# Three transfers instead of five for each block of raw weights, and the inverse root of the norms by logarithm and exponential instead of a power: a fused attention and SwiGLU kernel

## The chip, the cores and the metric

The kernel runs on one core of one Trainium2 chip. The metric is the device time of one execution in microseconds; a smaller time is better. A core has TensorE (PE in the profile; PEld is its weight load), VectorE (DVE), ScalarE (ACT), GpSimd (POOL) and SyncE (SP). Each has its own queue of instructions, worked off in order, and waits for the others by semaphores. SP only begins transfers (DMAs) here; ScalarE and GpSimd can begin some too.

## The reference

```python
# 8 batches, 12 heads, 448 positions, 64 values a head
def rmsnorm(x, g):
    rms = np.sqrt(np.mean(x * x, axis=-1, keepdims=True) + 1e-06)
    return x / rms * g
q_n, k_n = (rmsnorm(q, g_q), rmsnorm(k, g_k))
scores = 1.0 / np.sqrt(64) * np.matmul(q_n, k_n.transpose(0, 1, 3, 2))
attn = np.exp(scores - np.max(scores, axis=-1, keepdims=True))
attn = attn / (np.sum(attn, axis=-1, keepdims=True) + 1e-09)
x = np.matmul(attn, v)         # then laid out as 3584 tokens x 768
# gate and value weights 768 x 1536, output weights 1536 x 768
g = x @ w_gate
return (g * (1.0 / (1.0 + np.exp(-g))) * (x @ w_val)) @ w_out
```

The step that the change touches is `1 / rms`, the inverse root, for each row of q and k.

## The kernel before

The three weights arrive as 64-bit numbers, and the kernel turns them into 32-bit numbers itself. The large products are not done as written. Each is cut into 3 x 3 blocks and done with 15 smaller products in place of 27; for that, sums and differences of blocks ("sides") are needed of the weights and of the tokens. So a piece of weights goes through a *conversion* (`convert`): a load of nine raw blocks, two ScalarE activations (L1129, L1133), six VectorE instructions that round the numbers (L1151 to L1163), twelve GpSimd sums and differences of blocks (L1182, L1185), and a transfer of all 15 sides to DRAM (L1210), to `up_sides` (gate and value weights) or `down_sides` (output weights). There are 24 conversions: 16 of gate and value weights, 8 of output weights. Four blocks (`BLOCKS`) are sides as they are, the other eleven are made. Later `load_sides` (L1271) fetches the sides in the order in which the products use them, five at a time for the hidden products and two at a time for the output products, with one transfer for each run of neighbours.

Attention works on 48 *pairs* (two heads of one batch each, six pairs a batch), twelve pairs for each block of two batches. For each pair (`attention(m)`) the queue of work is:

- q and k are loaded by four transfers each (L702), v by four (L718, L721);
- ScalarE squares both (L728), VectorE sums the squares of rows (L742), ScalarE swaps halves between partitions (L752), VectorE adds the two and a small constant (L756), which gives `ss`, 128 partitions x 28 sums;
- the inverse root `rr` of these 28 sums: one GpSimd power (L767);
- GpSimd multiplies k and q by `rr` (L778, one instruction each), VectorE transposes them (L794), ScalarE multiplies q by both gains (L797);
- TensorE makes scores (L823), ScalarE exponentials (L838), TensorE weighted sums (L899) and row sums of the exponentials (L930). In later blocks GpSimd and VectorE first add the exponentials up (L843, L849);
- a reciprocal (L965), its spread over partitions (L973 or L983), and the join and division into `xs` (L988, L991, L995). VectorE then makes the token sides (L1032, L1036).

The buffers of q and k hold two pairs, so the loads of a pair wait for the pair two before it.

The stages follow each other like this: twelve early pairs beside six conversions; the hidden products of block 0 (L1311, with their reads L1253 to L1259, Silu L1385 and the weighing L1388) beside the other 18 conversions; then in turn for each block the output products (L1485) mixed with the twelve pairs of the next block, and the hidden products of that block; at the end the output products of block 3 alone.

The order on every queue is not written by hand. The class `Order` takes pieces of work with an engine, an estimated duration, a due time and dependencies, simulates the engines with these estimates, and emits each engine's instructions in the order that the simulation chose. The chip then works each queue strictly in that order. A piece of ScalarE's may name a `mode`, the table set it needs; a change of mode is booked at 1.3 us. The estimates and lines that matter here:

```python
rr = add("POOL", 0.5, ready - 14.0, roots, after=[sums], uses=[("ss", m)], takes=[("rr", m)])
# scale: "POOL", 1.0 each;  transpose: "DVE", 0.62;  queries: "ACT", 0.65
loaded = add("SP", 2.5, when - 12.0, load, after=[staged.get(place), *wait], kb=1152, early=3.0)
```

`by_bank` is false for the first six conversions, those among the early pairs, and true for the other 18. The tables are set to hold logarithm and exponential together (`natural_log_exp_and_others`, loaded in `load_tables`, L552); Silu needs another set, loaded before L1385.

Of the kernel before, what the change touches and what calls it, by code (L numbers as in the profile page):

```python
# [477 lines left out]
def fast(  # L478
# [41 lines left out]
    nc = tc.nc  # L520
# [3 lines left out]
    P = 128  # L524
# [15 lines left out]
    const = ctx.enter_context(tc.tile_pool(name="const", bufs=1))  # L540
# [7 lines left out]
        rr=4, ws=2, **{x + str(i): 1 for x in "vw" for i in range(6)},  # L548
# [5 lines left out]
    order = Order(BUFS, dict(logarithms=load_tables))  # L554
    tiles = {}

    WORK, size = {}, 0
# [48 lines left out]
    FRESH = (2, 6, 8, 12, 9)  # L606


    UP_SUMS = (8, 1, 7, 13, 10, 14, 3, 5, 11, 0, 4)
    DOWN_SUMS = (1, 10, 14, 3, 11, 0, 4, 5, 8, 7, 13)  # L610
    BLOCKS = (6, 2, 12, 9)
    WS = 10 * NC2 * P
    up_sides = [dram.tile([P, 15, 2, NC2, P], F32, name=f"up_sides{g}") for g in range(NG)]
    down_sides = dram.tile([P, 15, 2, NG, P], F32, name="down_sides")
# [17 lines left out]
    minus_half = const.tile([P, 1], F32, name="minus_half")  # L632

# [31 lines left out]
    down_products = {}  # L665


    SCALE = 2.0**8
    SPREAD = 6.0

    NC = S // C
    clusters = {}
# [4 lines left out]
    def attention(m):  # L677
# [53 lines left out]
        for x in range(2):  # L731
# [3 lines left out]
                    after=[loaded[x], *squares], uses=[("qk", (m, x))] + [("t", m)] * x,  # L735
                    takes=[("t", m)] * (1 - x),
# [25 lines left out]
        )  # L762
        sums = add("ACT", 0.9, ready - 16.0, swap, after=[sums], uses=[("ss", m)])
        sums = add("DVE", 0.15, ready - 15.0, both, after=[sums], uses=[("ss", m)])

        def roots():
            nc.gpsimd.tensor_tensor(  # L767
                out=take("rr", m, [P, 2 * NC]), in0=tiles["ss", m][:, 0],
                in1=minus_half.to_broadcast([P, 2 * NC]), op=ALU.pow,
            )  # L770

        rr = add(
            "POOL", 0.5, ready - 14.0, roots, after=[sums], uses=[("ss", m)], takes=[("rr", m)]
        )

        def scale(x):
            rr = tiles["rr", m][:, ts(x, NC)].rearrange("p (c one) -> p c one", one=1)
# [18 lines left out]
        def queries():  # L796
# [7 lines left out]
            uses=[("t", m)],  # L804
# [298 lines left out]
    def convert(key, src, sums, to, when, place, by_bank):  # L1103

        rank = 20.0 if by_bank else 0.0

        def add(*what, **more):
            return order.add(*what, **dict(rank=rank, **more))

        raw, dst = places[place][:, 0 : 2 * VALUES], places[place][:, 2 * VALUES : PLACE]  # L1110
        words = raw.bitcast(U32).rearrange("p (n two) -> p n two", two=2)
        lo, hi = words[:, :, 0], words[:, :, 1]
        wait = [last_exp[0]] if place in (ES, PAIRS, GT[2]) else []

        def load():

            to = raw.bitcast(I64).rearrange("p (b f) -> p b f", f=P)
            for i, n, rows in ((0, 2, (1, 3, 0)), (2, 2, (0, 2, 2)), (5, 3, (0, 3, 1))):
                nc.sync.dma_start(to[:, i : i + n], src(slice(*rows[:2]), rows[2]))
            for i, k, n in ((4, 0, 0), (8, 2, 2)):  # L1120
                nc.sync.dma_start(to[:, i], src(k, n))

        loaded = add(
            "SP", 2.5, when - 12.0, load, after=[staged.get(place), *wait], kb=1152, early=3.0
        )
        bits = dst.bitcast(U32)
# [12 lines left out]

        def half(k):  # L1140
            part = ts(k, VALUES // 2)
            if not by_bank:
                return part, bits[:, part]
            bank_of = tiles[bank].rearrange("p b t -> p (b t)")
            return part, bank_of[:, 0 : VALUES // 2].bitcast(U32)

        def shift(k):
            if by_bank and k == 0:
                take(*bank, [P, 2, TB])
            part, to = half(k)  # L1150
            nc.vector.tensor_scalar(  # L1151
                out=to, in0=bits[:, part], scalar1=3, scalar2=None, op0=ALU.logical_shift_left
            )

        def sign(k):
            part, to = half(k)
            nc.vector.scalar_tensor_tensor(
                to, hi[:, part], 0x80000000, to, op0=ALU.bitwise_and, op1=ALU.bitwise_or
            )

        def round_part(k):
            part, to = half(k)
# [12 lines left out]
        b21, b31, b13, b23, b11, b12, b22, b32, b33 = (blocks[:, i] for i in range(9))  # L1175

        sides = places[place].rearrange("p (b f) -> p b f", f=P)[:, 7:22]
        at = {x: i for i, x in enumerate(sums)}
        w = {x: sides[:, i] for x, i in at.items()}

        def minus(to, one, two):
            return lambda: nc.gpsimd.tensor_tensor(out=to, in0=one, in1=two, op=ALU.subtract)  # L1182

        def plus(to, one, two):
            return lambda: nc.gpsimd.tensor_tensor(out=to, in0=one, in1=two, op=ALU.add)  # L1185

        def pair(x, i, j):
            return x[:, i : j + 1 : j - i]

        def twice(x):  # L1190
            return x.rearrange("p (one f) -> p one f", one=1).to_broadcast([P, 2, P])

        for us, op in (
            (0.79, plus(pair(sides, at[10], at[4]), pair(blocks, 5, 7), pair(blocks, 2, 8))),
            (0.79, plus(pair(sides, at[1], at[14]), twice(w[10]), pair(blocks, 0, 4))),
            (0.48, plus(w[14], w[14], b31)),
            (0.48, minus(w[13], b22, w[10])),
            (0.48, minus(w[8], w[4], b23)),
            (0.48, plus(w[7], b21, b22)),
            (0.48, minus(w[7], w[8], w[7])),  # L1200
            (0.48, minus(w[3], b13, b31)),
            (0.48, minus(w[5], b13, b21)),
            (0.48, plus(w[5], w[5], b11)),
            (0.79, minus(pair(sides, at[11], at[0]), pair(blocks, 7, 8), pair(blocks, 2, 3))),
            (0.48, plus(w[0], w[0], b31)),
        ):
# [66 lines left out]

    def place_of(x, part, sums):
        mine = [*(y for y in sums if y in part), *(y for y in BLOCKS if y in part)]
        return mine.index(x)

    def block(n):
        add = order.add
# [292 lines left out]


    nc.gpsimd.memset(many, SCALE)
    nc.gpsimd.memset(minus_half, -0.5)
    nc.gpsimd.memset(halves, 0.0)
    for x in range(2):
        nc.gpsimd.memset(halves[ds(D * x, D), x], SCALE)
# [7 lines left out]
    for i in range(P // C):  # L1586
# [95 lines left out]
```

## Time and profile before

| | us |
|---|---|
| median of 3 runs | 1596.77 (1596.45 to 1597.97) |
| the profiled execution | 1596.45 |
| its span, first to last instruction | 1594.7 |
| PE busy | 1468.6 (92%) |
| VectorE busy | 896.1 (56%) |
| ScalarE busy | 657.3 (41%) |
| GpSimd busy | 644.1 (40%) |
| mean granted TensorE clock | 0.965 of full speed |
| moved by DMA | 193.29 MB |

The profile is of one execution. A group's line gives the code line, the engine, the operation, output and inputs with their shapes, the count, the busy time in us and the mean of one in ns, and after the bar how long the engine had been idle just before these instructions and what ended most of that. In a line of the timeline come the start, the length, the engine and the code line, and in brackets the idle time before and its releaser. A line of the waits names the waiting engine and instruction, what it waited for, the sum in us, how often, and the longest. In the table of stages come the stretch and its length, then the busy time of each engine with its instructions, the granted TensorE clock, the DMA share (mean busy share of the 16 DMA engines) and GB/s.

### The profile page before, as it was taken

Reading aid. Unit: us, or ns where it says so; the run is one execution under the profiler, and the core shown is the slowest. Engines: PE = TensorE matmul, PEld = TensorE weight load, DVE = VectorE, ACT = ScalarE, POOL = GpSimd, SP = SyncE. Lnnn points to the kernel's source line nnn. Section 1 sums busy time; section 2 is a strip of 40 time slices with the busy share of each in tenths; the row PEclk is TensorE's granted clock in tenths of the full one; section 3 lists DMA queues with packets and bytes.
Section 4 is the critical chain, followed back from the end, with each engine's and each line's share of the span. In section 5 each row is a group of like instructions: output and inputs, shape, how many; then the busy total and the mean of one; then the engine's idle time right before and its main releaser. Section 6 shows DMA issues by size and latency. Waiting matters only on the chain.

```text
span 1594.7 us, 19324 instructions
## 1 busy us (share of the span) xinstructions
PE 1468.6 (92%) x6672; PEld 688.4 (43%) x6672; DVE 896.1 (56%) x1261; ACT 657.3 (41%) x1264; POOL 644.1 (40%) x517
## 2 busy tenths in 40 slices
PE   4787889996888899999998999999998989999998
PEld 1333445442333345544443345554443434555554
DVE  2566887775674754443676764334676673333543
ACT  4574344334656332134665432234665532222100
POOL 5786757647856510034476610033377620000000
PEclk9898999998998999999998999999999999999999
DMA  5664899982433242253344251253344343222235
GB/s 110 139 147 108 274 305 353 290 259 61 97 82 75 71 106 99 95 118 104 76 107 101 59 125 67 99 136 89 83 108 87 83 90 110 87 79 99 80 91 100
DMA packets 415920, 193.29 MB, mean 121 GB/s; under 512 B 324164, under 2 KB 397892, under 8 KB 409668
## 3 DMA queue, kind: packets, MB, share of 16 engines
q1 hardware_dynamic: 402688, 190.35, 44.6%
q10 hardware_dynamic: 12996, 1.61, 0.7%
q8 instruction: 55, 0.90, 0.2%
q14 instruction: 53, 0.43, 0.1%
q0 software_dynamic: 128, 0.00, 0.0%
HBM read 157.29 MB, written 34.60 MB: 120 GB/s over the span
## 4 chain that ended last, share of the span: by engine, by line
PE 54%; DVE 8%; issue 6%; ACT 4%; POOL 3%; SPq 2%; DMA 2%; DVEq 0%; ACTq 0%; POOLq 0%
PE mm L1311 17%; PE at L1311 17%; PE mm L1485 13%; PE st L823 3%; PE at L899 2%; ACT spare L983 2%; POOL sums L843 2%; DVE xs L1036 1%; DVE rd L965 1%; SPq L702 1%; DVE sums L849 1%; POOL work L778 1%; ACT es L838 1%; DVE work L794 1%; DVE xs L995 1%
## 5 line engine op out<-in xcount | busy, mean ns | idle before, releaser
L1311 PE MATMUL mm<-xs,ws 128*128 128x448 f32 x960 | 401.9, 541 | 7.9 <-DMA ws<-up_sides 4.3
L767 POOL TENSOR_TENSOR rr<-ss,minus_half 128x28 f32<-128x28 f32 x48 | 237.2, 4941 | 414.6 <-DVE ss L756 406.9
L1311 PE MATMUL at<-xs,ws 128*128 128x448 f32 x960 | 402.7, 542 | 1.4 <-DVE v L1257 1.0
L1311 PEld LDWEIGHTS mm<-xs,ws 128*128 128x128 f32 x960 | 181.7, 190 | 189.6 <-issue 175.5
L1311 PEld LDWEIGHTS at<-xs,ws 128*128 128x128 f32 x960 | 183.0, 191 | 183.1 <-issue 173.2
L823 PE MATMUL st<-work 64*64 64x448 f32 (+1 forms) x1536 | 174.8, 561 | 92.0 <-ACT work L797 60.5
L1485 PE MATMUL mm<-gt,ws 128*128 128x448 f32 x448 | 186.3, 568 | 0.0
L1485 PE MATMUL mm<-hs,ws 128*128 128x448 f32 x384 | 155.3, 556 | 0.0
L794 DVE STREAM_TRANSPOSE work<-work 128x448 f32<-128x448 f32 x96 | 60.7, 636 | 162.8 <-POOL work L778 156.7
L838 ACT ACTIVATE es<-st 128x896 f32<-128x896 f32 x129 | 114.7, 914 | 67.3 <-PE at L899 39.4
L843 POOL TENSOR_TENSOR sums<-es 128x896 f32<-128x896 f32 x36 | 76.0, 2110 | 160.9 <-ACT xs L988 61.3
L823 PEld LDWEIGHTS st<-work 64*64 64x64 f32 x1536 | 53.0, 143 | 181.2 <-ACT work L797 68.5
L1255 DVE TENSOR_TENSOR gt<-gt,mm 128x448 f32<-128x448 f32 x64 | 39.6, 618 | 159.3 <-PE mm L1311 158.3
L983 ACT COPY spare<-rd 32x224 f32<-32x224 f32 x288 | 108.1, 375 | 50.0 <-DVE rd L965 43.7
L1485 PEld LDWEIGHTS mm<-gt,ws 128*128 128x128 f32 x448 | 87.4, 200 | 93.5 <-issue 90.8
L1385 ACT ACTIVATE st<-gt 128x448 f32<-128x448 f32 x96 | 52.4, 547 | 181.4 <-DVE gt L1259 83.2
L899 PE MATMUL at<-es,v 64*64 64x448 f32 x1032 | 110.2, 541 | 5.7 <-DVE xs L991 5.5
L1485 PEld LDWEIGHTS mm<-hs,ws 128*128 128x128 f32 x384 | 73.0, 195 | 75.3 <-issue 74.1
L1253 ACT COPY gt<-mm 128x448 f32<-128x448 f32 x80 | 42.5, 532 | 146.3 <-PE mm L1311 146.3
L778 POOL TENSOR_TENSOR work<-work,rr 128x448 f32<-128x448 f32 x96 | 97.1, 1030 | 3.5
L1253 ACT COPY v<-at 128x448 f32<-128x448 f32 x96 | 51.0, 532 | 80.5 <-PE at L1311 79.6
L843 POOL TENSOR_TENSOR sums<-sums,es 128x896 f32<-128x896 f32 x36 | 79.6, 2212 | 2.7
(147 smaller groups left out, 1570.9 us busy)
## 6 DMA issues: line engine op xcount, KB each, us to landing
ws<-up_sides SPq DMA_DIRECT2D x32, 1024.0 KB, 5.0
ws<-down_sides SPq DMA_DIRECT2D x16, 1024.0 KB, 4.9
ws<-down_sides SPq DMA_DIRECT2D x28, 512.0 KB, 4.3
ws<-up_sides SPq DMA_DIRECT2D x16, 768.0 KB, 4.4
work<-in_q_dram SPq DMA_DIRECT2D x192, 56.0 KB, 2.4
work<-in_k_dram SPq DMA_DIRECT2D x188, 56.0 KB, 2.5
out_dram<-spare SPq DMA_DIRECT2D x168, 56.0 KB, 1.9
v<-in_v_dram SPq DMA_DIRECT2D x96, 96.0 KB, 2.4
```

The lines of the kernel that those rows point to most:

```text
L767: nc.gpsimd.tensor_tensor(out=take("rr", m, [P, 2 * NC]), in0=tiles["ss", m][:, 0], in1=minus_half.to_broadcast([P, 2 * NC]), op=ALU.pow,)
L778: nc.gpsimd.tensor_tensor(out=tiles["t", m][:, x], in0=tiles["qk", (m, x)], in1=rr.to_broadcast([P, NC, C]), op=ALU.mult,)
L794: nc.vector.transpose(to, tiles["t", m][:, x].rearrange("p c f -> p (c f)"))
L823: nc.tensor.matmul(st[ds(D * x, D), h, 0:n], tiles["KT", m][rows, ds(P * j + D * of_keys, D)], tiles["QT", m][rows, ds(Q * of_queries, n)] ...
L838: nc.scalar.activation(e, tiles["st", (m, j)][:, :, 0 : S * width(j) // P], AF.Exp)
L843: nc.gpsimd.tensor_tensor(out=to, in0=tiles["e", (m, 0)] if j == 1 else to, in1=e, op=ALU.add)
L899: nc.tensor.matmul(tiles["at", (m, x)][ds(D * h, D), queries], tiles["v", m][rows, j, h], tiles["e", (m, j)][rows, h], start=j == 0, stop= ...
L983: nc.scalar.copy(inv[ds(D * h + C * to, C), ts(x, Q)], tiles["rd", m][ds(D * h + C * x, C)])
L1253: nc.scalar.copy(to, ps)
L1311: nc.tensor.matmul(ps(), w[:, at, which, c], xs[:, SLOT[x], c], start=fresh and c == 0, stop=c == NC2 - 1, skip_group_check=True,)
L1385: nc.scalar.activation(take(*act, [P, 2, TB])[:, 0, 0:S], to, AF.Silu)
L1485: nc.tensor.matmul(banks[s][:, 0:S], w[:, at, s, g], where[x][:, g], start=fresh and g == 0, stop=g == NG - 1, skip_group_check=True,)
```

## The change

The inverse root is made by two ScalarE activations, logarithm and then exponential of minus half of it, and three VectorE instructions that improve the result by one step of iteration. The sums are scaled by a power of two before the logarithm, and the product of the gains (`gg`) makes up for it. The power and its constant `minus_half` go.

The nine blocks of a raw weight come in three transfers of three blocks instead of two of two blocks, one of three and two of one. For that the rounded blocks lie ahead of the raw ones instead of behind, in another order, and so do the 15 sides: `BLOCKS` first, then the sums, both reordered; `load_sides` and `place_of` follow, and the same twelve GpSimd sums are written with the new places. For the first six conversions (`by_bank` false) GpSimd begins the three transfers, with 3.0 us booked on its queue; for the others SP does, with 1.5 us for 2.5.

```diff
-    UP_SUMS = (8, 1, 7, 13, 10, 14, 3, 5, 11, 0, 4)
-    DOWN_SUMS = (1, 10, 14, 3, 11, 0, 4, 5, 8, 7, 13)
-    BLOCKS = (6, 2, 12, 9)
+    UP_SUMS = (10, 14, 3, 8, 1, 7, 13, 5, 11, 0, 4)
+    DOWN_SUMS = (3, 10, 14, 1, 11, 0, 4, 5, 8, 7, 13)
+    BLOCKS = (6, 9, 2, 12)
...
+    def inverse_root(m, sums, of, when, rank=0.0):
+        def estimate():
+            ss = of()
+            rr = take("rr", m, list(ss.shape))
+            nc.scalar.activation(rr, ss, AF.Ln, scale=GAIN**-2)
+            nc.scalar.activation(rr, rr, AF.Exp, scale=-0.5)
+
+        def improve():
+            ss, rr = of(), tiles["rr", m]
+            times = nc.vector.scalar_tensor_tensor
+            times(ss, rr, GAIN**-2, ss, op0=ALU.mult, op1=ALU.mult)
+            times(ss, ss, -0.5, rr, op0=ALU.mult, op1=ALU.mult)
+            times(rr, ss, 1.5, rr, op0=ALU.add, op1=ALU.mult)
+
+        first = order.add(
+            "ACT", 0.5, when, estimate, after=[sums], uses=[("ss", m)], takes=[("rr", m)],
+            mode="logarithms", rank=rank,
+        )
+        return order.add(
+            "DVE", 0.45, when + 1.0, improve, after=[first], uses=[("ss", m), ("rr", m)],
+            rank=rank,
+        )
...
-        def roots():
-            nc.gpsimd.tensor_tensor(
-                out=take("rr", m, [P, 2 * NC]), in0=tiles["ss", m][:, 0],
-                in1=minus_half.to_broadcast([P, 2 * NC]), op=ALU.pow,
-            )
-
-        rr = add(
-            "POOL", 0.5, ready - 14.0, roots, after=[sums], uses=[("ss", m)], takes=[("rr", m)]
-        )
+        rr = inverse_root(m, sums, lambda: tiles["ss", m][:, 0], ready - 14.0, rank)
...
-        raw, dst = places[place][:, 0 : 2 * VALUES], places[place][:, 2 * VALUES : PLACE]
+        dst, raw = places[place][:, 0:VALUES], places[place][:, VALUES:PLACE]
...
-            for i, n, rows in ((0, 2, (1, 3, 0)), (2, 2, (0, 2, 2)), (5, 3, (0, 3, 1))):
-                nc.sync.dma_start(to[:, i : i + n], src(slice(*rows[:2]), rows[2]))
-            for i, k, n in ((4, 0, 0), (8, 2, 2)):
-                nc.sync.dma_start(to[:, i], src(k, n))
+            queue = nc.sync if by_bank else nc.gpsimd
+            for at, n in ((slice(3, 8, 2), 0), (slice(0, 3), 1), (slice(8, 3, -2), 2)):
+                queue.dma_start(to[:, at], src(slice(0, 3), n))

         loaded = add(
-            "SP", 2.5, when - 12.0, load, after=[staged.get(place), *wait], kb=1152, early=3.0
+            "SP" if by_bank else "POOL", 1.5 if by_bank else 3.0, when - 12.0, load,
+            after=[staged.get(place), *wait], kb=1152, early=3.0,
         )
...
-        b21, b31, b13, b23, b11, b12, b22, b32, b33 = (blocks[:, i] for i in range(9))
-
-        sides = places[place].rearrange("p (b f) -> p b f", f=P)[:, 7:22]
-        at = {x: i for i, x in enumerate(sums)}
+        b12, b22, b32, b11, b33, b21, b23, b31, b13 = (blocks[:, i] for i in range(9))
+
+        sides = places[place].rearrange("p (b f) -> p b f", f=P)[:, 5:20]
+        at = {x: i for i, x in enumerate((*BLOCKS, *sums))}
...
-        for names, first in ((sums, 0), (BLOCKS, len(sums))):
-            here = sorted(names.index(x) for x in part if x in names)
-            if here:
-                size = len(here)
-                src = sides[:, ds(first + here[0], size)]
-                nc.sync.dma_start(to[:, ds(i, size)], src.rearrange("p x a b f -> p x (a b f)"))
-                i += size
+        here = sorted((*BLOCKS, *sums).index(x) for x in part)
+        while here:
+            size = next((n for n in range(1, len(here)) if here[n] != here[0] + n), len(here))
+            src = sides[:, ds(here[0], size)]
+            nc.sync.dma_start(to[:, ds(i, size)], src.rearrange("p x a b f -> p x (a b f)"))
+            i += size
+            here = here[size:]
...
-            out=gg, in0=gq2, scalar=8.0, in1=gk2, op0=ALU.mult, op1=ALU.mult
+            out=gg, in0=gq2, scalar=8.0 * GAIN**-2, in1=gk2, op0=ALU.mult, op1=ALU.mult
```

More of the change, by code (lines that the diff above doesn't have):

```diff
@@ L631, in fast @@
     gg = const.tile([P, 1], F32, name="gg")
-    minus_half = const.tile([P, 1], F32, name="minus_half")
     LEAD, PAIR = 14.0, 9.0
@@ L665, in fast @@
     down_products = {}
+    GAIN = 2.0**24
     SCALE = 2.0**8
     SPREAD = 6.0
+    def inverse_root(m, sums, of, when, rank=0.0):
[18 more added lines that the diff above has]
+        )
     NC = S // C
@@ L1187, in pair @@
         def pair(x, i, j):
-            return x[:, i : j + 1 : j - i]
+            return x[:, i : j + (1 if j > i else -1) : j - i]
         def twice(x):
@@ L1193, in convert @@
         for us, op in (
-            (0.79, plus(pair(sides, at[10], at[4]), pair(blocks, 5, 7), pair(blocks, 2, 8))),
-            (0.79, plus(pair(sides, at[1], at[14]), twice(w[10]), pair(blocks, 0, 4))),
+            (0.79, plus(pair(sides, at[10], at[4]), pair(blocks, 0, 2), pair(blocks, 8, 4))),
+            (0.79, plus(pair(sides, at[14], at[1]), twice(w[10]), pair(blocks, 3, 5))),
             (0.48, plus(w[14], w[14], b31)),
@@ L1203, in convert @@
             (0.48, plus(w[5], w[5], b11)),
-            (0.79, minus(pair(sides, at[11], at[0]), pair(blocks, 7, 8), pair(blocks, 2, 3))),
+            (0.79, minus(pair(sides, at[11], at[0]), pair(blocks, 2, 4), pair(blocks, 8, 6))),
             (0.48, plus(w[0], w[0], b31)),
@@ L1265, in load_sides @@
         i = 0
-        for names, first in ((sums, 0), (BLOCKS, len(sums))):
-            here = sorted(names.index(x) for x in part if x in names)
-            if here:
-                size = len(here)
-                src = sides[:, ds(first + here[0], size)]
-                nc.sync.dma_start(to[:, ds(i, size)], src.rearrange("p x a b f -> p x (a b f)"))
-                i += size
+        here = sorted((*BLOCKS, *sums).index(x) for x in part)
[5 more added lines that the diff above has]
+            here = here[size:]
     def place_of(x, part, sums):
-        mine = [*(y for y in sums if y in part), *(y for y in BLOCKS if y in part)]
-        return mine.index(x)
+        return [y for y in (*BLOCKS, *sums) if y in part].index(x)
     def block(n):
@@ L1574, in fast @@
     nc.gpsimd.memset(many, SCALE)
-    nc.gpsimd.memset(minus_half, -0.5)
     nc.gpsimd.memset(halves, 0.0)
```

## The prediction

> **What bounds the kernel now.** I read the page's summary by engine first (PE busy 92% of the span, GpSimd 40%), then cut the span into its stages and asked for busy time, granted clock and DMA share in each: the early pairs (0 to 157 us), the first hidden stage with most conversions of weights (157 to 361), the first stage in which attention pairs and output products alternate (361 to 580), and so on in turn.
>
> ```profile
> core 0: us, PE busy (x) PEld busy (x) DVE busy (x) ACT busy (x) POOL busy (x), PEclk, DMA share, GB/s
> 0.00:157.00 157.00, 107.69 (x1112) 45.76 (x1116) 79.91 (x125) 88.71 (x156) 109.93 (x97) 0.90 0.56 127
> 157.00:361.00 204.00, 193.33 (x576) 96.66 (x566) 163.60 (x244) 83.26 (x114) 125.80 (x240) 0.98 0.93 291
> 361.00:580.00 219.00, 185.08 (x1100) 76.88 (x1100) 136.38 (x165) 115.31 (x249) 137.48 (x60) 0.91 0.36 79
> ...
> 769.00:949.00 180.00, 168.72 (x1054) 73.28 (x1053) 121.43 (x149) 102.01 (x218) 104.41 (x46) 0.95 0.41 91
> ```
>
> PE is idle for 157 - 107.7 = 49.3 us in the first stage, 10.7 in the second, 33.9 in the third, and 11.3 in the stage at 769. The twin stage at 1136 to 1317 has 12.0, the other hidden stages (580, 949, 1317) under 1 each. So most of what can be won lies in stages one and three. Next I read who waits there (stage one, then stage three):
>
> ```profile
> DVE work L794 <- POOL work L778: 50.0, 20, 5.9
> PE st L823 <- ACT work L797: 37.5, 9, 18.5
> ```
>
> ```profile
> DVE work L794 <- POOL work L778: 33.8, 12, 5.2
> PE st L823 <- ACT work L797: 15.0, 2, 9.7
> ```
>
> PE waits for the queries (L797), they for the transposes (L794), these for GpSimd's scaling (L778), and in front of that stands the power:
>
> ```profile
> L767 POOL TENSOR_TENSOR rr<-ss,minus_half 128x28 f32<-128x28 f32 x48 | 237.2, 4941 | 414.6 <-DVE ss L756 406.9
> ```
>
> It takes 4.94 us on 28 elements a partition, although the planner that orders all queues books 0.5 us for it. So the transpose is queued on VectorE as if it were due at once, and whatever is queued behind it waits too. The timeline of one pair (GpSimd's line, then VectorE's, then PE's) shows it:
>
> ```profile
> 58.44 4.79 POOL L767 TENSOR_TENSOR rr<-ss,minus_half 128x28 f32<-128x28 f32 x1 [7.06 <-DVE ss L756]
> ...
> 64.28 0.65 DVE L794 STREAM_TRANSPOSE work<-work 128x448 f32<-128x448 f32 x1 [5.92 <-POOL work L778]
> ...
> 66.36 0.58 DVE L991 TENSOR_TENSOR xs<-xs,at 128x448 f32<-128x448 f32 x1
> ...
> 67.00 1.01 PE L899 MATMUL at<-es,v 64*64 64x448 f32 x2 [5.14 <-DVE xs L991]
> ```
>
> VectorE stands 5.92 us, the join L991 behind it comes late, and PE stands 5.14 us for that join. Stage three begins the same way:
>
> ```profile
> 362.79 4.80 POOL L767 TENSOR_TENSOR rr<-ss,minus_half 128x28 f32<-128x28 f32 x1 [15.23 <-DVE ss L756]
> ...
> 370.93 2.52 PE L823 MATMUL st<-work 64*64 64x224 f32 x16 [9.73 <-ACT work L797]
> ```
>
> Of PE's 9.73 us without work, 4.80 are the power. From 362.8 to 528.7 the twelve powers follow each other every 15.1 us, and one turn near 452 can be followed: GpSimd's two sums (4.4), VectorE's own sum and a read (1.9), row sums (1.1), ScalarE's swap (0.9), VectorE's combination and L756 (2.2), the power (4.8), one scaling (0.9), about 16 us. The power is a third of that loop.
>
> **The inverse root.** Removed: 48 powers, 237.2 us of GpSimd. Added for each pair: two ScalarE activations of 28 elements a partition (nearest row: a copy of 32x28, 212 ns, so 0.42), three VectorE instructions of the shape of L756 (median 189 ns, mean 316, so 0.57 to 0.95), and two more crossings between engines (58.36 to 58.44 in the rows above, 0.08, so 0.2). From L756 to the first scaling that makes 1.2 to 1.6 us; I take 1.5 for 4.94, a gain of 3.4 a pair. That is the best end. The other end: the new ScalarE pieces can stand behind two exponentials (2 x 0.91) and the VectorE pieces behind a reciprocal (1.5), and then 1.5 + 1.8 + 1.5 = 4.8 gains nothing. I take the gain's end, because the new costs are planned at 0.5 and 0.45, near those rows, so what is queued behind them arrives when it can run, which was not so for the power.
>
> Stage one: the nine waits of PE for the queries are one of 18.5 at the start and eight that sum to 19.0 (2.4 each). The first shrinks by 3.4, the eight by some 2 each: 20 us. Ends: 0, and 3.4 + 19.0 + the 5.1 of L991 = 27.5.
>
> Stage three: the loop falls to 15.1 - 3.4 = 11.7 us a pair, under what PE needs (185.1 / 12 = 15.4), so PE is next. It should then idle as at 769 (11.3) plus the start, 9.7 - 3.4 = 6.3: 185.1 + 17.6 = 202.7, a gain of 16. The granted clock is 0.91 here and 0.95 at 769; if the closer work brings it to 0.95, PE's 185.1 become 177.3, 8 more. Together 24; ends 0 and 39 (as short as the stage at 769, 180).
>
> The alternating stages at 769 and 1136: PE waits 4.0 for the queries in each. I take 3 each, 6 in all; ends 0 and 8. Stage two has no pairs, and the tail after 1317 has neither.
>
> Against this stand tables. Logarithm and exponential share the table set that the exponentials use, but in the hidden stages at 580 and 949 four pairs are prepared between Silu activations. Powers begin at 685.6, 701.8, 722.2 and 731.8, Silus run before, between and after the first two, and the set is now loaded only at 732.1. The first two pairs would add a load there and back: 4 loads in each of two stages, 8 x 1.283 = 10.3 us of ScalarE, which is busy 59.7 of 189 us there. Ends for PE: 0 and 10.3; I take 2, because each result bank is read some 6 us apart and a copy takes 0.53. The row for such a switch, and the next activation after it:
>
> ```profile
> 370.90 1.28 ACT L552 ACT_TABLE_LOAD   x1
> 372.19 0.54 ACT L838 ACTIVATE more<-st 128x448 f32<-128x448 f32 x1
> ```
>
> The next activation starts at once. The Trainium skill ("ScalarE: Activation LUTs", What ACT_TABLE_LOAD costs) states 2.66 us for every switch, a drain of 1.38 included; by that the eight would be 21.3 us of ScalarE, and my term for PE perhaps 4. The trace shows no such drain after the load.
>
> **The transfers.** Five transfers a conversion become three; bytes and pieces stay. SP spends 0.47 us on an issue (median at L1119), so 18 later conversions save 36 issues, 17 us of a queue that stage two does not wait for: the DMA share there is 0.93, and transfers, not issues, are full. Value 0, ends 0 and 5. The new order of sides makes the five sides of a hidden load 5 transfers a group for 6, and leaves the output loads at 11: 0. GpSimd's sums keep number and shape: 0.
>
> The first six conversions' loads, 18 transfers, leave SP for GpSimd's queue. On SP they took 2.6 us a conversion; SP waits there for free buffers, so nothing is won. On GpSimd the only rows are small:
>
> ```profile
> 1.39 0.72 POOL L1583 DMA_DIRECT2D gq<-in_g_q_dram  x1
> 2.11 0.53 POOL L1584 DMA_DIRECT2D gq<-in_g_q_dram  x1
> ```
>
> 64 pieces took 0.53 us; a transfer has now 128 x 3 = 384. Ends: 0.53 each, 9.5 us in all, and six times that, 3.2 each, 57 us. I take 1 us, 18 in all, by the fixed part. GpSimd was busy 110 of 157 us in stage one; less 59 of powers, plus 18, leaves 69. Queued behind a load are scalings and side sums, and for a scaling wait its transposes and PE. Half of six loads in front of a scaling at 3 us, mostly inside the 5 us of room per pair that the powers leave: 2 us lost.
>
> A rule speaks against this part. The Trainium skill ("SBUF — State Buffer", SBUF: two separate sides) says that VectorE in its two-port modes locks GpSimd out of writing descriptors, so a load begun there stalls. No row of this trace has such a load beside such an instruction, and my term stays as it is.
>
> **The sum.** 20 + 24 + 6 - 2 - 2 = 46. The profiled execution took 1596.45 us (span 1594.7, 1.75 around it), the median of the runs 1596.77, so the two can be used alike: 1596.45 - 46 = 1550.5.
>
> **Rivals.** *Loads in the power's place* (0.14): a GpSimd load costs by its pieces. Then 57 us stand where 59 were, in six lumps of 9.6, and stage one gains nothing: 1570. For: the same queue, the same scalings behind it. Against: the loads need no data and can go where GpSimd idles.
>
> *The wait only moves* (0.08): ScalarE's and VectorE's queues eat the 3.4, and only a little is left of the start: 1590.
>
> *Slower* (0.10): the logarithm waits in ScalarE's queue for L756, and exponentials that PE needs are queued behind it. GpSimd's waits for L756 (406.9 us) hurt nobody; ScalarE already waits 1.5 us on average for row sums (38.8 in 26) and VectorE 0.8 for the swap (19.5 in 24). A second such exchange, 2.3 us a pair, in the 24 pairs of the alternating stages at 769 and 1136, where PE has under 1 us a pair to spare, costs 55; with the 4 above, less 44 of the early gains, the time is 15 us up, 1611. It decides from (20 + 24 - 4) / 24 = 1.7 us a pair. Against: in those stages PE waits only 6.3 us for exponentials, so ScalarE has room.
>
> **How the numbers follow.** The forecast has 0.68; its own range is 1530 to 1572. To 1570 and 1590 go 0.14 and 0.08, so the high end is 1588; the low end, 1528, needs most of the upper ends of stages one and three (27 + 39). A measurement here can tell about 0.2% (3 us) from no change. Faster: 0.68 + 0.14 + half of 0.08 = 0.86; the other half is no change, 0.04; slower 0.10.
>
> **What would show it.** Right: no L767; VectorE's wait for L778 from 50 to under 25 us in stage one and from 34 to under 15 in stage three; the first hidden product near 144 rather than 164.0; the second hidden stage's first near 539 rather than 582.8; 24 table loads for 16. Wrong: GpSimd's loads over 2 us each with scalings late behind them; ScalarE waiting for L756 for over 50 us with PE waiting for exponentials; the stages at 769 and 1136 longer than 181.

## The result and the profile after

The changed kernel takes 1516.67 us (median of 4 runs, 1515.84 to 1517.92) against 1596.61 before: ratio 0.9499, 95% interval 0.9482 to 0.9515. The profiled execution's span is 1516.1 us at a mean granted clock of 0.986. The forecast was 1550.5 with a range of 1528 to 1588: the sign was right, the time lies 11 us below the range.

The table of stages of the changed kernel, cut at the first product of each stage (columns as in the table shown of before):

```profile
core 0: us, PE busy (x) PEld busy (x) DVE busy (x) ACT busy (x) POOL busy (x), PEclk, DMA share, GB/s
0.00:159.67 159.67, 112.11 (x1196) 48.21 (x1197) 100.64 (x174) 95.30 (x183) 82.17 (x126) 0.93 0.72 168
159.67:354.90 195.23, 185.94 (x486) 92.20 (x485) 151.07 (x230) 81.59 (x116) 110.57 (x216) 0.98 0.86 268
354.90:536.08 181.18, 172.43 (x1105) 72.62 (x1105) 138.33 (x205) 118.31 (x270) 80.72 (x48) 0.98 0.45 98
721.60:886.47 164.87, 162.17 (x1057) 71.58 (x1056) 124.77 (x176) 105.30 (x234) 64.97 (x38) 1.00 0.45 100
```

GpSimd is lighter in every stage where it works, but the early stage is still 159.67 long, 47.6 of it without PE work. The alternating stage of the last line has little idle time left (2.7 us), and its granted clock went from 0.95 to 1.00. (In the table below, `hidden` are the stages of hidden products, `alt.` those in which output products and pairs alternate; stage three of the prediction is `alt. 0`.) Cut in the same way, the stages of both profiled kernels are (us):

| | early | hidden 0 | alt. 0 | hidden 1 | alt. 1 | hidden 2 | alt. 2 | hidden 3 | tail |
|---|---|---|---|---|---|---|---|---|---|
| before | 164.0 | 197.2 | 221.6 | 185.6 | 182.1 | 185.7 | 180.2 | 180.7 | 97.6 |
| changed | 159.7 | 195.2 | 181.2 | 185.5 | 164.9 | 185.5 | 164.7 | 180.7 | 98.7 |
| gain | 4.3 | 2.0 | 40.4 | 0.1 | 17.2 | 0.2 | 15.5 | 0.0 | -1.1 |

The waits that the prediction named, early stage first (0 to 159.67), then stage three (354.9 to 536.08):

```profile
DVE work L811 <- POOL work L795: 1.1, 2, 0.8
PE st L840 <- ACT work L814: 27.1, 5, 21.4
```

```profile
DVE work L811 <- POOL work L795: 4.1, 6, 1.1
PE st L840 <- ACT work L814: 2.8, 1, 2.8
```

VectorE hardly stands for GpSimd's scaling in either any more (50.0 and 33.8 before). In stage three PE's wait for the queries went with it, from 15.0 to 2.8. In the early stage one wait of 21.4 us remains at the start, longer than the 18.5 of before. The new steps of pair 0, from the combined sums to the first scaling (timeline rows of VectorE, ScalarE, VectorE, GpSimd):

```profile
9.94 0.19 DVE L782 SCALAR_TENSOR_TENSOR ss<-ss 128x28 f32<-128x28 f32 x1 [0.95 <-ACT ss L778]
...
10.16 0.23 ACT L678 ACTIVATE rr<-ss 128x28 f32<-128x28 f32 x1 [0.25 <-DVE ss L782]
10.42 0.23 ACT L679 ACTIVATE rr<-rr 128x28 f32<-128x28 f32 x1
...
11.12 0.19 DVE L686 SCALAR_TENSOR_TENSOR rr<-ss,rr 128x28 f32<-128x28 f32 x1
...
11.53 0.93 POOL L795 TENSOR_TENSOR work<-work,rr 128x448 f32<-128x448 f32 x1 [3.33 <-DMA work<-in_k_dram]
```

From the end of the combined sums (L782, 10.13) to the scaling at 11.53 are 1.4 us; the estimate was 1.5. That is an undisturbed pair. Over all 48, the way from the end of the combined sums to the end of the inverse root is 2.05 us in the median and 2.5 in the mean, at most 6.5 (L782 to L686); before it was 4.88 in the median and 5.2 in the mean (L756 to L767). So each pair gained some 2.8 us, less than the 3.4 of the forecast, and both questions lie elsewhere: why the inverse root was worth far more than forecast, and why the early stage did not shrink.

### The profile page after: what moved, and what is told of

Its sections match the earlier page's. It is cut to its first block, busy times and chain, and to the rows that moved or that the text cites. A ratio compares the mean times of both kernels' runs of the same rounds, so it can differ in the third digit from the quotient of the medians.

```text
span 1516.1 us, 19383 instructions
## 1 busy us (share of the span) xinstructions
PE 1436.6 (95%) x6672; PEld 678.5 (45%) x6672; DVE 914.1 (60%) x1405; ACT 679.9 (45%) x1364; POOL 427.3 (28%) x486
## 4 chain that ended last, share of the span: by engine, by line
PE 71%; DVE 4%; ACT 2%; issue 1%; SPq 1%; DMA 1%; DVEq 0%; ACTq 0%
PE mm L1501 21%; PE at L1327 18%; PE mm L1327 18%; PE st L840 6%; PE at L916 5%; PE st L947 1%; SPq L728 1%; ACT es L855 1%; ACT spare L1000 1%; DVE rd L982 0%; DMA out_dram<-spare 0%; DVE ss L782 0%; DMA down_sides<-hs 0%; DVE hs L1053 0%; DVE gt L1404 0%
## 5 line engine op out<-in xcount | busy, mean ns | idle before, releaser
L795 POOL TENSOR_TENSOR work<-work,rr 128x448 f32<-128x448 f32 x96 | 106.2, 1125 | 482.4 <-DVE rr L686 232.4
L840 PE MATMUL st<-work 64*64 64x448 f32 (+1 forms) x1536 | 160.3, 526 | 38.3 <-ACT work L814 29.9
L1501 PE MATMUL mm<-gt,ws 128*128 128x448 f32 x448 | 177.1, 545 | 0.0
L1272 DVE TENSOR_TENSOR gt<-gt,mm 128x448 f32<-128x448 f32 x64 | 39.7, 620 | 188.1 <-PE mm L1327 177.3
L1401 ACT ACTIVATE st<-gt 128x448 f32<-128x448 f32 x96 | 52.4, 547 | 175.7 <-DVE gt L1276 92.1
L1501 PEld LDWEIGHTS mm<-gt,ws 128*128 128x128 f32 x448 | 83.0, 190 | 83.8 <-issue 80.4
L768 DVE TENSOR_REDUCE ss<-work 128x28 f32<-128x896 f32 x48 | 51.6, 1075 | 42.8 <-ACT work L754 42.6
L811 DVE STREAM_TRANSPOSE work<-work 128x448 f32<-128x448 f32 x96 | 59.1, 627 | 24.5 <-POOL work L795 22.6
```

Of the source, the lines that this page charges most:

```text
L768: nc.vector.tensor_reduce(out=take("ss", m, [P, 2, 2 * NC])[:, 0], in_=tiles["t", m].rearrange("p x c f -> p (x c) f"), axis=AX.X, op=ALU.add,
L795: nc.gpsimd.tensor_tensor(out=tiles["t", m][:, x], in0=tiles["qk", (m, x)], in1=rr.to_broadcast([P, NC, C]), op=ALU.mult,)
L811: nc.vector.transpose(to, tiles["t", m][:, x].rearrange("p c f -> p (c f)"))
L840: nc.tensor.matmul(st[ds(D * x, D), h, 0:n], tiles["KT", m][rows, ds(P * j + D * of_keys, D)], tiles["QT", m][rows, ds(Q * of_queries, n)] ...
L1401: nc.scalar.activation(take(*act, [P, 2, TB])[:, 0, 0:S], to, AF.Silu)
L1501: nc.tensor.matmul(banks[s][:, 0:S], w[:, at, s, g], where[x][:, g], start=fresh and g == 0, stop=g == NG - 1, skip_group_check=True,)
```

## The experiments

The first four runs split the change. Their expectations speak of four theories. A: the length of the power in each pair's chain is the whole cost. B: the transfers give a part of the gain. C: what harms is the booking of 0.5 us for a step of 4.9, by the order of queues that follows from it. D: the raw loads that GpSimd begins collide with the loads of q and k among the first pairs.

**The inverse root alone**, on the kernel before:

```diff
-        rr = add("POOL", 0.5, ready - 14.0, roots, ...)          # the power
+        rr = inverse_root(m, sums, lambda: tiles["ss", m][:, 0], ready - 14.0, rank)
```

> The kernel before with the inverse root alone changed (logarithm, exponential, three VectorE instructions); raw weights still come in five transfers from SP. Theory A (the power's length in the loop of each pair was the whole cost, and the transfers do nothing): 1510 to 1525 us, with the alternating stages at 181, 165, 165 us as in the changed kernel. Theory B (the transfers gave a part of the 80 us): 1535 us or more. Theory D (the raw loads on GpSimd's queue collide with the loads of q and k among the early pairs and eat what the root wins there): early stage ends near 148 us instead of 159.7, so 1500 to 1510 us in all.

Measured: 1487.72 us, ratio 0.9314 (0.9298 to 0.9329). That is 29 us *less* than the whole change, and below what each of the theories A, B and D gave. The early stage is 140.7 long, alternating stages 175.9, 164.7, 164.9.

**The transfers alone**, on the kernel before, the power kept:

```diff
+    ... new UP_SUMS, DOWN_SUMS, BLOCKS, convert(), load_sides() of the change
         rr = add("POOL", 0.5, ready - 14.0, roots, ...)          # unchanged
```

> The kernel before with the transfers alone changed (three a conversion, the first six conversions' loads begun by GpSimd, the new order of sides); the power stays. Theory A: within 8 us of 1596.6. Theory B: 1570 us or less. Theory D: the early stage grows, 1600 to 1612 us.

Measured: 1608.81 us, ratio 1.0075 (1.0058 to 1.0091): the transfers by themselves are a loss of 12 us, the early stage 175.9 for 164.0. B falls, D stands.

**The changed kernel, its early raw loads begun by SP:**

```diff
-            queue = nc.sync if by_bank else nc.gpsimd
+            queue = nc.sync
-            "SP" if by_bank else "POOL", 1.5 if by_bank else 3.0, when - 12.0, load,
+            "SP", 1.5, when - 12.0, load,
```

> The changed kernel with the early raw loads, still three a conversion, begun by SP and booked there. Theory D: the loads of q and k are late no longer, the early stage shrinks by some 10 us, 1507 us. Theory B (GpSimd's begin helps, because SP's queue is held up among the early pairs): the early stage grows by 5 to 15 us, 1522 to 1532 us. Theory A: within 5 us of 1516.7.

Measured: 1506.47 us, ratio 0.9426 (0.9409 to 0.9443). The total is D's, but the early stage is 165.4, not shorter, and 19 us are still missing to the inverse root alone. So D was not all of it.

**The kernel before with the power booked at its length:**

```diff
-            "POOL", 0.5, ready - 14.0, roots, after=[sums], ...
+            "POOL", 4.9, ready - 14.0, roots, after=[sums], ...
```

> The kernel before with the power booked at 4.9 us instead of 0.5; nothing else differs but the order of instructions in the queues. Theory C (the harm is the wrong booking: VectorE is told to wait at the transposes and holds up what is queued behind): most of the gain comes back, 1530 to 1555 us. Theory A (the power's own 4.9 us in the loop and in GpSimd's time is the harm, whatever the order): 1580 to 1600 us.

Measured: 1537.91 us, ratio 0.9642 (0.961 to 0.9674), with the same instructions as before but for one table load each way, in another order. C is confirmed: 59 of the 109 us between before and the inverse root alone come from the order that the wrong booking made. The other 50 are what is left when the order knows the power's length, and they are not its length alone, as the stages show (us, profiled executions; the last two rows belong to runs further down):

| | early | hidden 0 | alt. 0 | alt. 1 | alt. 2 |
|---|---|---|---|---|---|
| before | 164.0 | 197.2 | 221.6 | 182.1 | 180.2 |
| power booked right | 166.8 | 190.2 | 181.0 | 172.0 | 172.3 |
| inverse root alone | 140.7 | 190.9 | 175.9 | 164.7 | 164.9 |
| unused power | 175.7 | 184.7 | 183.1 | 171.3 | 170.4 |
| hop | 159.4 | 197.9 | 180.2 | 170.2 | 169.8 |

The booking alone shortens `alt. 0` by 40.5 us, as much as the whole change did, and the early stage not at all. There the run booked right has a loss of its own: PE stands 18.65 us for the weights of the first hidden product. In SP's queue these stand behind raw loads (rows of SP, then PE), and SP had also waited 9.7 us for GpSimd's sums:

```profile
152.53 1.46 SPq L1119 DMA_DIRECT2D gt<-in_moe_w_gate_dram  x3
157.11 3.70 SPq L1271 DMA_DIRECT2D ws<-up_sides  x2
166.77 3.32 PE L1311 MATMUL mm<-xs,ws 128*128 128x448 f32 x4 [18.65 <-DMA ws<-up_sides]
```

So the 50 us are not the price of the longer chain alone. The two later alternating stages show 7.3 and 7.4 us of it each.

**Where the 19 us of the run with SP went.** SP's queue, timeline rows from 118 to 170 us of that run:

```profile
134.93 9.90 SPq L1137 DMA_DIRECT2D es<-in_moe_w_val_dram  x3
...
147.47 7.12 SPq L1137 DMA_DIRECT2D gt<-in_moe_w_gate_dram  x3
156.36 0.83 SPq L1287 DMA_DIRECT2D ws<-up_sides  x2
```

The weights `ws` of the first hidden product stand behind raw loads of the second batch, the first of which waited for its buffer; PE began that product at 165.38. These raw loads had moved forward because they were booked at 1.5 us for 2.5. The next run has the booking of before and nothing else:

```diff
-            "SP", 1.5, when - 12.0, load,
+            "SP", 2.5, when - 12.0, load,
```

> The changed kernel with the early raw loads begun by SyncE, three a conversion, booked 2.5 as five were booked before. Order theory: what the run with the booking of 1.5 lost (1506.5 against 1487.7 for the inverse root alone) comes from raw loads of the second batch that the shorter booking put ahead of the first hidden stage's weight loads in SyncE's queue; with 2.5 they stand behind them, so 1484 to 1494, the early stage 140 to 148 long (165.4 with 1.5). Layout theory: three long transfers of other blocks cost by themselves: 1500 or more, the early stage 155 or more.

Measured: 1490.25 us, ratio 0.9343 (0.9323 to 0.9364), the early stage 139.2. The same queue in this run:

```profile
124.24 1.30 SPq L1287 DMA_DIRECT2D ws<-up_sides  x3
126.60 0.57 SPq L1227 DMA_DIRECT2D up_sides<-hs  x1
132.30 6.91 SPq L1137 DMA_DIRECT2D es<-in_moe_w_val_dram  x3
```

The weights go first. Order theory holds: begun by SP and booked at 2.5, three transfers in the new layout cost and win next to nothing (2.5 us above the inverse root alone, with intervals that overlap).

**GpSimd's early loads behind pair 1's scaling.** In the changed kernel the first six transfers of raw weights have nothing in front of them in GpSimd's queue (rows of GpSimd, SP, ScalarE and PE):

```profile
3.64 4.57 POOL L1137 DMA_DIRECT2D xs<-in_moe_w_gate_dram  x6
...
8.61 3.90 SPq L744 DMA_DIRECT2D v<-in_v_dram  x2
...
17.90 0.58 ACT L754 ACTIVATE work<-work 128x448 f32<-128x448 f32 x1 [3.30 <-DMA work<-in_k_dram]
...
21.43 4.62 PE L840 MATMUL st<-work 64*64 64x224 f32 x32 [21.43 <-ACT work L814]
```

They fill the DMA engines (share 1.03 from 3.6 to 20 us, 0.80 with the inverse root alone); SP needs 3.90 us to begin two loads of v that take it 1.01 in the run with SP at 2.5, ScalarE waits 3.30 for a k, and PE begins at 21.43. With the inverse root alone PE begins at 14.74, and before at 18.53. The test moves the loads back:

```diff
-            after=[staged.get(place), *wait], kb=1152, early=3.0,
+            after=[staged.get(place), *wait, *([] if by_bank else [scale_done[1]])], ...
```

> The changed kernel, its early raw loads still begun by GpSimd, but behind GpSimd's scaling of the second pair in its queue instead of at 3.6 us. Collision theory: the raw transfers begun at 3.6 us take the DMA engines from the first pairs' q and k, which holds pair 1's squares back; behind the scaling the first scores start near 14.7 (21.4 in the changed kernel, 14.7 with the inverse root alone), and 1503 to 1511 in all. Theory that GpSimd as the beginner costs it, by its queue or its buffers: 1514 to 1520, and the first hidden stage still begins near 160.

Measured: 1508.02 us, ratio 0.9451 (0.9431 to 0.9472). PE's first scores start at 14.73, the early stage is 151.3. So the collision at the start is worth 9 us of the 29, as expected of it; another 18 against the run with SP at 2.5 remain. That run differs in a second point, though: it books the loads of the 18 later conversions, which SP begins in all these runs, at 2.5 too, and the changed kernel and this run book them at 1.5. How the 18 us divide between beginner and booking is not shown. SP's rows in this run show a like collision later, while transfers that GpSimd began at 17.6 to 24.5 are under way. The first fence has these rows, the second the like row with SP as the only beginner:

```profile
21.52 5.26 SPq L728 DMA_DIRECT2D work<-in_q_dram  x4
26.83 7.73 SPq L728 DMA_DIRECT2D work<-in_k_dram  x4
```

```profile
22.62 2.95 SPq L728 DMA_DIRECT2D work<-in_k_dram  x4
```

Undisturbed, four such issues take 1.9 us. With SP as the only beginner, four that follow its own raw loads took up to 4.10 us (at 36.40). Is it GpSimd, or any second beginner?

**Early raw loads begun by ScalarE:**

```diff
-            queue = nc.sync if by_bank else nc.gpsimd
+            queue = nc.sync if by_bank else nc.scalar
-            "SP" if by_bank else "POOL", 1.5 if by_bank else 3.0, when - 12.0, load,
+            "SP" if by_bank else "ACT", 1.5, when - 12.0, load,
```

> The changed kernel with the early raw loads begun by ScalarE, on its own queue, booked 1.5. Theory of two beginners (raw transfers begun by a second engine are no longer kept behind q, k and v by SyncE's written order, and take the DMA engines from them): as harmful as begun by GpSimd, 1503 to 1525, q and k landing late among the first pairs and SyncE's own issues slowed. Theory that GpSimd's way of beginning a transfer is the harm: 1484 to 1496, as begun by SyncE with 2.5.

Measured: 1504.05 us, ratio 0.9414 (0.9398 to 0.943). First scores at 18.33, against 14.60 with SP alone: at the start the theory of two beginners holds. The total is 14 us above the run with SP at 2.5, as that theory called for, but 2 us below the run with SP at 1.5, which books the later loads as this run does; so the 14 can't be put down to the second beginner. A part looks like the booking's: in the first hidden stage PE waits 6.0 us for `ws` here and 4.5 in the changed kernel, 1.3 with SP at 2.5. GpSimd is 12.6 us worse than ScalarE in its place, with the later loads booked alike; from which of its loads, and whether by its queue or its time, no run here separates. The Trainium skill ("DMA: Bandwidth & Descriptors", Issuing engines are not separate DMA queues) says that transfers begun by different engines run on the same 16 DMA engines and interleave there. The rows above agree, and show the price: while SP begins them all, the raw weights stand behind q, k and v of the first two pairs in the written order and begin at 12.10; GpSimd begins them at 3.64 and ScalarE at 4.21.

**Why the power cost so much.** Three runs ask what about the power harms. First, a short step in its place on GpSimd, a multiplication by a constant. This run leaves the inverse root out, so only its time counts:

```diff
-                in1=minus_half.to_broadcast([P, 2 * NC]), op=ALU.pow,
+                in1=minus_half.to_broadcast([P, 2 * NC]), op=ALU.mult,
...
-    nc.gpsimd.memset(minus_half, -0.5)
+    nc.gpsimd.memset(minus_half, 1.0 / 512)
```

> The kernel before with the power replaced by a multiplication by a constant of the same shape, on GpSimd, booked 0.5: the inverse root is left out. Theory that the power's length is the harm: as good as the inverse root on the two other engines, 1481 to 1492, alternating stages of 164 to 167, the early stage 138 to 144. Theory that a step on GpSimd between VectorE and GpSimd's own scaling is the harm, whatever its length: 1540 or more. Theory that the wrong booking is all: it is right here (a short step booked short), so below 1537.9.

Measured: 1487.57 us, ratio 0.9328 (0.931 to 0.9346). So a short step on GpSimd is as good as the inverse root on the two other engines: the length matters, and not that the step stands on GpSimd.

Second, the inverse root on the two other engines, and an unused power per pair behind the scalings:

```diff
+        def idle():
+            nc.gpsimd.tensor_tensor(out=scratch, in0=many[:, 0:1].to_broadcast([P, 2 * NC]),
+                in1=minus_half.to_broadcast([P, 2 * NC]), op=ALU.pow)
+        add("POOL", 4.9, ready - 9.0, idle, after=[scaled[-1]])
```

> The kernel before with the inverse root on ScalarE and VectorE, and one more power per pair on GpSimd behind the scalings, booked 4.9, whose result nothing reads. Latency theory (the power harmed because each pair's chain waited for it): 1485 to 1495. Occupancy theory (it harmed because GpSimd was taken, so that the next pair's scaling, the gathering of sums or transfers came late, or because VectorE shares its port): 1510 to 1545, most of what the power cost when it was booked right (1537.9).

Measured: 1541.49 us, ratio 0.9669 (0.9648 to 0.969). Latency theory falls in its narrow form: a power whose result nobody reads costs 54 us, about as much as the real one when it is booked right. As in that run, a part is a wait of PE for the first weights (22.16 us at 175.66); the alternating stages show 5.5 to 7.2 us each.

```profile
13.38 4.82 POOL L812 TENSOR_TENSOR scratch<-many,minus_half 128x28 f32<-128x28 f32 x1
18.18 1.83 POOL L798 TENSOR_TENSOR work<-work,rr 128x448 f32<-128x448 f32 x2
```

It stands in GpSimd's queue in front of the next pair's scaling, so it lengthens that pair's chain. VectorE is also longer busy beside it, 135.6 us for 124.5 in `alt. 1`; what that costs no run separates.

Third, the opposite: a longer chain that holds hardly any engine. One small transfer of the sums from one place of SBUF to another, before the logarithm:

```diff
+        def hop():
+            nc.scalar.dma_start(ss[:, 1], ss[:, 0])
+        sums = add("ACT", 0.6, ready - 14.5, hop, after=[sums], ...)     # planned at 2.5 more
-        rr = inverse_root(m, sums, lambda: tiles["ss", m][:, 0], ready - 14.0, rank)
+        rr = inverse_root(m, sums, lambda: tiles["ss", m][:, 1], ready - 14.0, rank)
```

> The kernel before with the inverse root on ScalarE and VectorE, and between the sums and the logarithm of each pair one more small transfer of the sums from one place of SBUF to another, begun by ScalarE and planned at 2.5 us: it lengthens each pair's chain by about the 3.4 us that the power was longer than the new steps, and takes next to nothing of any engine but its issue on ScalarE. Occupancy theory (the power harmed because it held GpSimd): within some 12 us of 1487.7, alternating stages of 164 to 167. Latency theory, as predicted (the power harmed because each pair's chain waited for it): 1510 to 1540, alternating stages of 169 or more.

Measured: 1530.96 us, ratio 0.9585 (0.9564 to 0.9607), inside what latency theory expects and far outside the other. The transfers of that line from 723 to 893 us:

```profile
DMA to landing us min/median/max: 1.7/1.9/3.7
```

With the wait in ScalarE's queue, the way from the combined sums to the inverse root grew from 2.07 to 6.28 us in the median of the 48 pairs (2.8 to 6.1 in the mean; 5.5 with the power booked right). This, with 0.47 us of ScalarE for each issue, cost 43 us. So each of the two theories holds in its own run: a longer chain of a pair costs time whether a wait lengthens it or what stands in front of it in a queue. How the 50 us of a rightly booked power divide between its own pair and the next stays open, since here every power does both.

How the delay reaches PE is in ScalarE's wait for the transposes in the stage `alt. 1` (768 to 950 before): before; changed; power booked right; unused power; hop; multiplication.

```profile
ACT work L797 <- DVE work L794: 21.6, 5, 6.4
```

```profile
ACT work L814 <- DVE work L811: 3.5, 2, 2.5
```

```profile
ACT work L797 <- DVE work L794: 15.1, 4, 8.6
```

```profile
ACT work L825 <- DVE work L822: 11.9, 3, 7.2
```

```profile
ACT work L823 <- DVE work L820: 14.9, 4, 8.4
```

```profile
ACT work L797 <- DVE work L794: 2.2, 2, 1.9
```

The lengths of that stage, in the same order: 182.1, 164.9, 172.0, 171.3, 170.2, 162.2. While ScalarE stands at the queries of the coming pair, the exponentials of the present pair are queued behind it, and PE waits for those: before, 6.3 us of PE's wait in this stage were for exponentials (first fence below), and after it is 0.6 (second). One turn of before shows the whole chain (ScalarE, ScalarE, PE):

```profile
864.74 0.67 ACT L797 ACTIVATE work<-work,gg 128x448 f32<-128x448 f32 x1 [6.31 <-DVE work L794]
865.32 1.71 ACT L838 ACTIVATE es<-st 128x896 f32<-128x896 f32 x2
866.27 0.62 PE L823 MATMUL st<-work 64*64 64x224 f32 x8 [3.50 <-ACT es L838]
```

```profile
PE st L823 <- ACT es L838: 6.3, 7, 3.5
```

```profile
PE st L840 <- ACT es L855: 0.6, 2, 0.4
```

## Why the prediction was wrong, by its steps

The step that failed is the price of the power: 3.4 us a pair of its own length, read from PE's own wait for the queries. The order that its booking of 0.5 us made had no term in the sum, and the stages at 769 and 1136, which suffer from the same power, were taken as nearly free of it. The runs show 59 us for the order alone, and 17.2 and 15.5 us in those two stages where 3 each stood.

*The chain* was right, and VectorE's wait for the scaling fell to 1.1 and 4.1, where under 25 and under 15 were called for. Its length was right in an undisturbed pair (1.4 us for 1.5) and too short in the median (2.05): the gain was some 2.8 us a pair and not 3.4. So the length was not under-priced by its size in us, but by what a us of it costs.

*Stage one, 20 us:* the term is right for the inverse root alone, 164.0 - 140.7 = 23.3. In the changed kernel 4.3 are left, since the transfers took 19.0 back. The sign given for it, the first hidden product near 144, was missed: 159.67.

*Stage three, 24 us, measured 40.4.* What failed here is "it should then idle as at 769 (11.3)", with the clock of 769 for the rest and that stage's 180 as the end of the range. The sum had 177.3 busy and 17.6 idle; measured are 172.4 and 8.8. The stage at 769 was no floor: it suffered from the same power. With the power kept and only booked right this stage is 181.0: of the 45.7 us by which the inverse root alone shortens it, the order makes 40.5.

*The alternating stages, 3 us each, measured 17.2 and 15.5.* "PE waits 4.0 for the queries" was read as all that the power cost there. In the first of them idle time fell from 12.0 to 2.7 and busy time from 170.1 to 162.2. The 7.9 of busy time go with the granted clock: 170.1 x 0.95 = 161.6 and 162.2 x 1.00 = 162.2 are nearly the same work. The idle time includes the 6.3 for exponentials behind ScalarE's stand, which the prediction used as a sign that ScalarE has room. The range broke here: its end of 8 for both stages stood where 32.7 came.

*The booking.* The prediction saw that the order was planned for 0.5 us and named VectorE's queue as the victim, but priced only the power's length, 3.4 a pair. The order itself was the larger part, 59 of 109 us: 40.5 in `alt. 0`, 10.1 and 7.9 in the two later alternating stages.

*Tables, -2:* both hidden stages stayed as long as they were (185.6 to 185.5, 185.7 to 185.5). 20 loads, not 24:

```profile
L552 ACT ACT_TABLE_LOAD x10 | 12.8, 1283 | 1.8 <-PEq L1681 1.6
L1401 ACT ACT_TABLE_LOAD x10 | 12.8, 1283 | 0.2
```

*The transfers, -2, measured -29* (1516.67 against 1487.72; on the kernel before, -12). The counting of GpSimd's time was not at fault: an issue took 0.758 us where 1 was taken, 13.6 in all, and the rival of loads in the power's place, which needed far longer ones, didn't come. What was missing: the transfers themselves. "The loads need no data and can go where GpSimd idles" is just what sent them off at 3.64 us, ahead of the second pair's k (5.36) and of v (8.61) on the DMA engines. The step "SP waits there for free buffers, so nothing is won" looked at SP's time alone, and not at the order that SP kept. The new booking of SP's loads was not priced either; in the run with SP it alone was worth 16 us (1506.5 to 1490.3).

*The errors had opposite signs:* the inverse root was worth 109 us, not 48, and the transfers cost 29, not 2. The second hidden stage's first product at 536.08, near the forecast 539, looks like a hit and is the sum of both.

*The slower rival:* ScalarE's logarithms did wait for the combined sums, but 20.4 us in all, and PE's waits for exponentials (`es`) fell from 25 to 12 us.

## What to carry to other kernels

Where queues are ordered by a planner, first compare each booked duration with the profile: here a step booked at a tenth of its length cost more by the order it made (59 us) than by all that was left of it in the right order (50 us), and one changed number shows it. Price a late step not by PE's wait for it alone but by everything queued behind the engine that stands for it, and do not take a stage that has the same step for the floor. A transfer moved to another engine leaves the order it was kept in: ask what it will overtake on the DMA engines, not only what its issue costs.

Both the inverse root alone (1487.72) and all of the change with SP as the beginner at 2.5 us (1490.25) beat the changed kernel: the part of the change that earns its time is the inverse root.

## What the runs showed of the hardware

- A small VectorE instruction of two inputs took up to eleven times its median length. L782 of the changed kernel took 0.188 us in the median and 2.087 at most. In the run with the hop (rows of GpSimd, then VectorE) one ends with GpSimd's sum:

```profile
747.55 2.08 POOL L869 TENSOR_TENSOR sums<-sums,es 128x896 f32<-128x896 f32 x1
...
747.76 1.91 DVE L785 SCALAR_TENSOR_TENSOR ss<-ss 128x28 f32<-128x28 f32 x1
```

The Trainium skill ("SBUF — State Buffer", SBUF: two separate sides) says that such a VectorE instruction and a GpSimd one that reads SBUF exclude each other for a whole instruction, whichever starts first. The row agrees: 747.76 + 1.91 and 747.55 + 2.08 end within 0.05 us. In the chain of a pair the new VectorE steps run that risk too (L684 took up to 1.615 us for 0.186), which the sum of 1.5 us did not hold.

- The same page's warning that the prediction weighed, that VectorE can hold up a transfer begun by GpSimd, is not seen in the issues: the 18 took 0.758 to 0.809 us each. What slowed was SP: 7.73 us for four issues that take 1.9, in the run with GpSimd's loads behind pair 1's scaling.

- The granted clock rose as idle time left the alternating stages: 0.92 in the stage `alt. 0` of before (PE busy 84%), 0.95 in `alt. 1` of before (93%), 0.99 with the hop (97%), 1.00 in the changed kernel (98%). In `alt. 1` 9.3 us of idle time and 7.9 of busy time went together. The busy share alone does not set it: with the power booked right `alt. 0` has 1.00 at 94%, and the early stage of the run with the multiplication 0.99 at 78%. What does, no run here separates.
